# The clamp and the shift-and-mask of the float64 weights' conversion: once over 1024 columns or twice over 512

## The chip, the cores and the metric

The kernel runs on one core of one Trainium2 chip. The metric is the device time of one execution in microseconds (us). A core has TensorE (PE: matrix products; PEld: its weight loads), VectorE (DVE), ScalarE (ACT), GpSimd (POOL), and SyncE (SP), whose queue starts most of the transfers.

## The reference

Three layers follow each other: a cross read between tokens and state rows, a gated linear unit, and a soft mixture of experts. The expert weights and the attention are left out here but for their shapes; what the change touches are `w_gate`, `w_val` and `w_out`, which come as float64, since a float32 draw is multiplied by a float64 scalar.

```python
def _attn_ref(x, state):                  # x (8, 8, 512, 64), state (8, 8, 32, 64)
    a = softmax(scale * x @ state.T); xread = a @ state
    a2 = softmax(scale * state @ x.T); sread = a2 @ x
    return concatenate([xread, sread], axis=2)
def _moe_ref(x, w_gate, w_val, w_out, rms_g):   # x (4608, 512) -> 4352 rows here, d_ff 1536
    rms = np.sqrt(np.mean(x * x, axis=-1, keepdims=True) + 1e-06)
    xn = x / rms * rms_g
    g = xn @ w_gate
    silu = g * (1.0 / (1.0 + np.exp(-g)))
    val = xn @ w_val
    return (silu * val @ w_out).astype(np.float32)
def _moe2_ref(x, phi, w1, w2):            # 8 experts of 4 slots
    logits = x @ phi
    d = softmax over tokens; slot_input = d.T @ x
    slot_out[e] = np.maximum(slot_input[e] @ w1[e], 0.0) @ w2[e]
    c = softmax over slots; return c @ slot_out
```

## The kernel before, in words

The tokens are worked through in eight groups of 512 (one for each batch) and one of 256 (the sread rows). A group's attention is kept as the pair "weights A, state rows", so that the gate and value products of a group are A times (state rows times weight chunk): `sw` (L430 and on) multiplies the state rows by a chunk of 512 weight columns and splits the product into two parts (ScalarE L442, VectorE L443), `main_mm` multiplies A by them, L471 and L479 make silu times value, `h_T` (L490) turns it and `lg_mm` multiplies it by w_out @ phi, which `wphi_part` builds from converted rows of w_out (L632, L635, L639). The weights' chunk that `sw` reads is `W[gv, c]`, a tile of 128 x 4 x 512.

The weights arrive as the two 32-bit words of each float64 (`wload`, tile `raw`, 2 x 128 rows of 512 weights a load), and are rounded to float32 on the chip. There are 24 such half-chunks: 12 for the gate and value weights (out tile `w`), 6 of w_out's transpose and 6 of w_out (out tile `wo`); the last six are written to a tensor in the chip's memory for the tail. A conversion has two steps. `wconv_begin` is two ScalarE instructions over 1024 columns: the high word's magnitude (L184) and the scaled low word (L187). `wconv` is the rest: a clamp (VectorE, L200), a shift with a mask (VectorE, L204), a merge with the high word's upper bits (VectorE, L208), and an add of the rounded low word (GpSimd, L212). All four run on 512 columns at a time, first the one half, then the other.

What sets the order: the start-up, from the first load to the first group's norm, lies in a block whose order on each engine is that of the program text. It holds four conversions, each between pieces of the first group's attention, and on VectorE in this order: conversion, row maxima of the scores (L251) and of their transposes (L272, L273), conversion, sums and products of the softmax (L298 to L308), the split of the first product (L443), conversion, the two differences of A (L380), conversion, the split of the second product (L443), the norm's Newton steps (L409 to L422). GpSimd has the adds between the state's scaling (L227) and the state's mask product (L357, L365, L366). After the start-up a table (`at(unit, slot, function)`) sets the program text's order of conversions and all other pieces beside the main products; from it a scheduler makes each engine's order at compile time, by priority and readiness, so that neighbouring pieces interleave. In the steady stages one conversion belongs to a stage of 12 units.

Of the kernel before, what the change touches and what calls it, by code (L numbers as in the profile page):

```python
# [13 lines left out]
ALU = mybir.AluOpType  # L14
# [6 lines left out]
def kernel(  # L21
# [16 lines left out]
    nc = tc.nc  # L38
# [3 lines left out]
    DM = H * D  # L42
# [10 lines left out]
    big = ctx.enter_context(tc.tile_pool(name="big", bufs=1))  # L53
# [32 lines left out]

# [1 line left out]
    ident = small("ident", [P, P])  # L88
# [9 lines left out]

    # Bits of float64's high word, read as float32: the least and greatest that float32 holds.
    EXP_LO, EXP_HI = 2.0 ** -15, 122879.984375  # L100

    def keep_warm(n):
        """Products that nobody reads, so that a short wait doesn't slow the array's clock."""
        ps = mmps()
        for _ in range(n):
            tc.keep_in_program_order(nc.tensor.matmul(out=ps[:, :P], lhsT=ident, rhs=ident, start=True, stop=True))
# [3 lines left out]

# [1 line left out]
    XN, T = {}, {}  # L112
# [19 lines left out]

# [1 line left out]
    dram = ctx.enter_context(tc.tile_pool(name="dram", bufs=1, space=bass.MemoryType.DRAM))  # L134
# [57 lines left out]
    def wconv(n):  # L192
        for _ in range(n):
            if not begun:
                wconv_begin()
            gv, c, j, d2, dst, hi, rnd = begun.pop(0)
            a = dst.bitcast(I32)
            hs = [slice(0, 512), slice(512, 1024)]
            for h in hs:
                nc.vector.tensor_scalar(  # L200
                    out=dst[:, h], in0=dst[:, h], scalar1=EXP_LO, scalar2=EXP_HI,
                    op0=ALU.max, op1=ALU.min,
                )
                nc.vector.tensor_scalar(  # L204
                    out=a[:, h], in0=a[:, h], scalar1=3, scalar2=0x3FFFFFF8,
                    op0=ALU.logical_shift_left, op1=ALU.bitwise_and,
                )
                nc.vector.scalar_tensor_tensor(  # L208
                    out=a[:, h], in0=hi[:, h], scalar=-0x40000000, in1=a[:, h],
                    op0=ALU.bitwise_and, op1=ALU.bitwise_or,  # L210
                )
                nc.gpsimd.tensor_tensor(  # L212
                    out=a[:, h], in0=a[:, h], in1=rnd[:, h], op=ALU.add
                )
            if gv == 2:
                WOT[c, j] = d2
            if gv == 3:
                r0 = c * 512 + 2 * j * P
                nc.sync.dma_start(
                    out=w_out32[r0 : r0 + 2 * P, :].rearrange("(k p) d -> p k d", p=P), in_=d2  # L220
                )


# [1 line left out]
    def att_g(b):  # L225
# [177 lines left out]
    def rinv_from(g, ss, n):  # L403
        """(ss / DM + 1e-6) ** -0.5, by Newton's steps from the halved exponent."""
        y = small("rinv", [P, NT], bufs=3)[:, :n]
        v = small("rv", [P, NT])[:, :n]
        a = small("ra", [P, NT])[:, :n]
# [18 lines left out]

# [1 line left out]
    WP = {}  # L428
# [18 lines left out]

# [1 line left out]
    HH, HT, LGP = {}, {}, {}  # L449
# [60 lines left out]

# [1 line left out]
    sacc = small("sacc", [P, 1])  # L512
# [107 lines left out]

# [1 line left out]
    wphi_done, WPP = set(), {}  # L622

    def wphi_part(c, j):
        """phi' @ w_out' for half of the d_model rows of a 512-wide chunk; j = 1 ends the chunk."""
        wt = WOT.pop((c, j))
# [16 lines left out]

# [1 line left out]
    def sread_prep():  # L645
# [27 lines left out]
    def w_split(gv, c):  # L673
        """The weights' chunk in two float32r parts."""
        w = W.pop((gv, c))
        h, l = k8("wh", F32R), k8("wl", F32R)
# [6 lines left out]

# [1 line left out]
    EW = {}  # L685
# [14 lines left out]
    def prefetch(n, home=None):  # L700
        """Start the next n loads, in slots of `big` (home None) or of the experts' pool."""
        for _ in range(n):
# [23 lines left out]

# [1 line left out]
    def conv1(n=1):  # L728
# [43 lines left out]
    pinned.append(1)  # L772
# [1 line left out]
    def rinv(b):  # L774
# [24 lines left out]
    for s, units in enumerate(stages):  # L799
# [66 lines left out]
        else:  # L866
            g = s
            o = 4 if s == 1 else 0  # the first unit's place in the usual twelve
            if s == 1:
# [125 lines left out]

# [1 line left out]
    h_T(*pend[0])  # L997
# [59 lines left out]
    for k in range(4):  # L1057
        mm(ps[:, 32 * k : 32 * k + 32], sip[:, k * P : (k + 1) * P], r32)
    # each expert's inputs of its own slots, zero in the others'
    for e in range(NE):  # L1060
# [20 lines left out]
    def expert_in(p):  # L1081
        """The first products of two experts: slots of one have zeros in the other."""
        for j in range(2):
# [39 lines left out]
    def out_prep():  # L1123
        """Group 0's weights of the slots, in two parts, each four times."""
        ch = k8("ch", F32R)[:, 0, :P].rearrange("p (t s) -> p t s", s=32)
# [87 lines left out]

    # so_ps still has the four parts of each slot's sum; group 0 takes it as it is
    s4 = k8("s4", F32R)
# [88 lines left out]
```

## Time and profile before

| | us |
|---|---|
| runs, median (lowest to highest of 3) | 690.29 (690.04 to 691.79) |
| profiled execution, span | 691.4 |
| TensorE busy in it | 640.3 (93%) |
| VectorE, ScalarE, GpSimd busy | 407.7, 388.9, 129.1 |

A line of the timeline gives start, length, engine, line, operation, tile written and read, shapes, how many were merged into the line, and in brackets how long the engine stood idle before it and who released it. Instructions on one engine can overlap a little at their ends, so the length of two merged ones is less than twice one. PEclk is the clock that was granted to TensorE: 1.00 is 2.4 GHz, 0.50 is 1.2 GHz.

### The profile page before, as it was taken

Reading aid. Unit: us, or ns where it says so; the run is one execution under the profiler, and the core shown is the slowest. Engines: PE = TensorE matmul, PEld = TensorE weight load, DVE = VectorE, ACT = ScalarE, POOL = GpSimd, SP = SyncE. Lnnn points to the kernel's source line nnn. Section 1 sums busy time; section 2 is a strip of 40 time slices with the busy share of each in tenths; the row PEclk is TensorE's granted clock in tenths of the full one; section 3 lists DMA queues with packets and bytes.
Section 4 is the critical chain, followed back from the end, with each engine's and each line's share of the span. In section 5 each row is a group of like instructions: output and inputs, shape, how many; then the busy total and the mean of one; then the engine's idle time right before and its main releaser. Section 6 shows DMA issues by size and latency. Waiting matters only on the chain.

```text
span 691.4 us, 11529 instructions
## 1 busy us (share of the span) xinstructions
PE 640.3 (93%) x4560; PEld 410.6 (59%) x4560; DVE 407.7 (59%) x852; ACT 388.9 (56%) x632; POOL 129.1 (19%) x158
## 2 busy tenths in 40 slices
PE   6789988999989999999999999999999999999980
PEld 4346646456555766566676658665666676753350
DVE  6979996762687457554835673575455355342160
ACT  5477943754776459546764765496446366311170
POOL 2634554230032101110201021011000000002430
PEclk9799998999999999999999999999999999999995
DMA  9940246031042011203110320020081307999957
GB/s 349 404 193 2 101 152 236 1 129 63 1 156 96 5 47 77 96 5 122 45 53 1 122 92 1 19 105 31 1 309 58 122 1 257 326 334 382 344 186 331
DMA packets 33581, 92.55 MB, mean 134 GB/s; under 512 B 1912, under 2 KB 4088, under 8 KB 30712
## 3 DMA queue, kind: packets, MB, share of 16 engines
q1 hardware_dynamic: 33240, 91.76, 36.3%
q8 instruction: 36, 0.59, 0.4%
q14 instruction: 17, 0.14, 0.1%
q10 hardware_dynamic: 288, 0.07, 0.0%
HBM read 79.76 MB, written 12.06 MB: 133 GB/s over the span
## 4 chain that ended last, share of the span: by engine, by line
PE 75%; DVE 7%; ACT 5%; issue 1%; POOL 0%; DVEq 0%; ACTq 0%
PE mm L85 42%; PE misc L85 17%; PE misc L109 10%; PE lg L85 3%; PE so L85 2%; DVE wp L443 1%; DVE h L479 1%; ACT wp L442 1%; ACT L471 1%; DVE wo L200 1%; ACT sg L471 1%; DVE wo L208 1%; DVE rm L272 1%; ACT sT L285 0%; DVE wo L204 0%
## 5 line engine op out<-in xcount | busy, mean ns | idle before, releaser
L85 PE MATMUL mm<-wp,A 128*128 128x512 f32 x1152 | 304.9, 405 | 0.4 <-DVE h L479 0.4
L85 PEld LDWEIGHTS mm<-wp,A 128*128 128x128 f32 x1152 | 207.3, 189 | 64.1 <-issue 24.5
L479 DVE SCALAR_TENSOR_TENSOR h<-mm,rinv,sg 128x512 f32<-128x512 f32 x102 | 76.1, 747 | 131.1 <-PE mm L85 93.6
L471 ACT ACTIVATE sg<-mm,rinv 128x512 f32<-128x512 f32 x102 | 70.2, 690 | 81.0 <-PE mm L85 78.0
L85 PE MATMUL misc<-w,stTg 64*32 64x512 f32 x768 | 81.7, 618 | 17.6 <-DVE wp L443 7.5
L442 ACT CAST wp<-misc 128x512 fp32r<-128x512 f32 x96 | 51.7, 591 | 65.2 <-PE misc L85 63.1
L443 DVE TENSOR_TENSOR wp<-misc,wp 128x512 fp32r<-128x512 f32 x96 | 61.8, 682 | 26.6 <-ACT wp L442 26.1
L109 PE MATMUL misc<-ident,h 128*128 128x128 f32 x408 | 61.3, 277 | 1.9 <-DVE h L479 0.7
L490 ACT COPY hT<-misc 128x512 f32<-128x512 f32 x86 | 49.2, 580 | 24.6 <-PE misc L109 20.5
L109 PEld LDWEIGHTS misc<-ident,h 128*128 128x128 f32 x408 | 50.1, 142 | 18.2 <-DVE wp L443 3.3
L85 PEld LDWEIGHTS misc<-w,stTg 64*32 64x32 f32 x768 | 15.5, 106 | 67.7 <-issue 22.1
L308 POOL TENSOR_TENSOR a<-a,asum 128x1024 f32<-128x1024 f32 x7 | 13.4, 1917 | 132.4 <-issue 84.8
L471 ACT ACT_TABLE_LOAD x28 | 35.9, 1283 | 3.7 <-PE mm L85 3.2
L416 POOL TENSOR_TENSOR rinv<-ri,rs_magic 128x4 int32<-128x4 int32 (+1 forms) x9 | 1.8, 198 | 173.2 <-DVE ri L412 173.2
L397 ACT ACTIVATE misc<-misc 128x512 f32<-128x512 f32 x32 | 18.7, 585 | 26.9 <-PE misc L85 18.8
L212 POOL TENSOR_TENSOR w<-w,raw 128x512 int32<-128x512 int32 x20 | 28.1, 1418 | 27.6 <-ACT wp L442 7.2
L85 PE MATMUL mm<-wh,xsg 128*128 128x512 f32 x96 | 31.7, 399 | 0.0
L85 PE MATMUL misc<-bd,A 128*128 128x256 f32 x192 | 29.6, 292 | 1.5 <-DVE A L380 1.5
L212 POOL TENSOR_TENSOR wo<-wo,raw 128x512 int32<-128x512 int32 x18 | 24.8, 1387 | 32.7 <-DVE wo L208 23.3
L85 PE MATMUL lg<-hT,wphi 128*32 128x512 f32 (+1 forms) x216 | 27.4, 577 | 1.5 <-ACT hT L490 1.5
L85 PEld LDWEIGHTS misc<-bd,A 128*128 128x128 f32 x192 | 25.5, 191 | 5.1 <-DVE A L380 2.2
L85 PE MATMUL misc<-h,ET 128*32 128x512 f32 x204 | 26.4, 596 | 0.0
(196 smaller groups left out, 831.8 us busy)
## 6 DMA issues: line engine op xcount, KB each, us to landing
ew<-in_w_dram SPq DMA_DIRECT2D x27, 1024.0 KB, 8.1
xT<-in_x_t_dram SPq DMA_DIRECT2D x8, 1024.0 KB, 5.5
xn<-in_x_n_dram SPq DMA_DIRECT2D x8, 1024.0 KB, 7.7
raw<-in_w_val_dram SPq DMA_DIRECT2D x6, 1024.0 KB, 16.6
raw<-in_w_out_dram SPq DMA_DIRECT2D x6, 1024.0 KB, 5.0
out_dram<-ob SPq DMA_DIRECT2D x6, 1024.0 KB, 12.1
ew_w<-in_w_dram SPq DMA_DIRECT2D x5, 1024.0 KB, 10.4
raw<-in_w_gate_dram SPq DMA_DIRECT2D x4, 1024.0 KB, 14.2
```

Of the source, the lines that this page charges most:

```text
L85: nc.tensor.matmul(out=o, lhsT=lhsT, rhs=rhs, start=start, stop=stop)
L109: nc.tensor.transpose(o, i, ident)
L200: nc.vector.tensor_scalar(out=dst[:, h], in0=dst[:, h], scalar1=EXP_LO, scalar2=EXP_HI, op0=ALU.max, op1=ALU.min,)
L208: nc.vector.scalar_tensor_tensor(out=a[:, h], in0=hi[:, h], scalar=-0x40000000, in1=a[:, h], op0=ALU.bitwise_and, op1=ALU.bitwise_or,)
L212: nc.gpsimd.tensor_tensor(out=a[:, h], in0=a[:, h], in1=rnd[:, h], op=ALU.add)
L308: (eng or nc.gpsimd).tensor_tensor(out=a3, in0=a3, in1=asum.unsqueeze(2).to_broadcast([P, 32, 32]), op=ALU.mult)
L397: nc.scalar.activation(out=ps, in_=ps, func=AF.Square, accum_out=T[b, "ss"][:, t : t + 1])
L442: nc.scalar.copy(t[:, r, 0, :], ps)
L443: nc.vector.tensor_tensor(out=t[:, r, 1, :], in0=ps, in1=t[:, r, 0, :].bitcast(F32), op=ALU.subtract)
L471: nc.scalar.activation(out=sg, in_=ps, func=AF.Silu, scale=RINV[g][:, t : t + 1])
L479: nc.vector.scalar_tensor_tensor(out=HH[g, c][:, t, :], in0=ps, scalar=RINV[g][:, t : t + 1], in1=sg, op0=ALU.mult, op1=ALU.mult,)
L490: (nc.vector.tensor_copy if on_dve else nc.scalar.copy)(HT[g, c][:, :, t * P : (t + 1) * P], ps.rearrange("p (q n) -> p q n", q=4))
```

## The change

The clamp and the shift-and-mask are taken out of the loop over the two halves and run once over all 1024 columns, before it. The merge and the add stay in the loop. Each conversion has thus two VectorE instructions fewer (six become four), and both halves' clamp and shift come ahead of the first merge in the program text. The diff also drops comments and docstrings, which are not shown.

```diff
             a = dst.bitcast(I32)
             hs = [slice(0, 512), slice(512, 1024)]
+            nc.vector.tensor_scalar(
+                out=dst, in0=dst, scalar1=EXP_LO, scalar2=EXP_HI,
+                op0=ALU.max, op1=ALU.min,
+            )
+            nc.vector.tensor_scalar(
+                out=a, in0=a, scalar1=3, scalar2=0x3FFFFFF8,
+                op0=ALU.logical_shift_left, op1=ALU.bitwise_and,
+            )
             for h in hs:
-                nc.vector.tensor_scalar(
-                    out=dst[:, h], in0=dst[:, h], scalar1=EXP_LO, scalar2=EXP_HI,
-                    op0=ALU.max, op1=ALU.min,
-                )
-                nc.vector.tensor_scalar(
-                    out=a[:, h], in0=a[:, h], scalar1=3, scalar2=0x3FFFFFF8,
-                    op0=ALU.logical_shift_left, op1=ALU.bitwise_and,
-                )
                 nc.vector.scalar_tensor_tensor(
                     out=a[:, h], in0=hi[:, h], scalar=-0x40000000, in1=a[:, h],
                     op0=ALU.bitwise_and, op1=ALU.bitwise_or,
```

## Rows read from the trace of the kernel before

**Rows 1.** The page: busy us (share) xinstructions of each engine; TensorE's busy tenths

```profile
PE 640.3 (93%) x4560; PEld 410.6 (59%) x4560; DVE 407.7 (59%) x852; ACT 388.9 (56%) x632; POOL 129.1 (19%) x158
...
PE   6789988999989999999999999999999999999980
```

**Rows 2.** Stretches: length, then busy us of PE, PEld, DVE, ACT, POOL; PEclk; DMA

```profile
80.00:90.00 10.00, 10.00 (x60) 7.48 (x59) 10.00 (x15) 7.89 (x11) 6.20 (x5) 1.00 0.84 315
110.00:120.00 10.00, 8.27 (x103) 5.71 (x109) 6.55 (x11) 1.91 (x3) 5.96 (x4) 0.83 0.41 142
329.00:393.00 64.00, 62.46 (x478) 41.84 (x477) 37.44 (x80) 40.62 (x67) 8.18 (x8) 1.00 0.17 60
```

**Rows 3.** The clamp's line for gate and value weights: ns shortest/median/longest

```profile
L200 DVE TENSOR_SCALAR w<-w x24: 366/420/2151, 7.1 to 89.1; 128x512 f32<-128x512 f32 x24
```

**Rows 4.** Timeline of the start-up's second conversion, VectorE and GpSimd

```profile
15.38 0.42 DVE L200 TENSOR_SCALAR w<-w 128x512 f32<-128x512 f32 x1
15.83 0.43 DVE L204 TENSOR_SCALAR w<-w 128x512 int32<-128x512 int32 x1
16.29 0.69 DVE L208 SCALAR_TENSOR_TENSOR w<-raw,w 128x512 int32<-128x512 int32 x1
...
17.12 1.35 POOL L212 TENSOR_TENSOR w<-w,raw 128x512 int32<-128x512 int32 x1 [4.32 <-DVE w L208]
17.36 1.40 DVE L204 TENSOR_SCALAR w<-w 128x512 int32<-128x512 int32 x1
...
19.40 0.16 DVE L298 TENSOR_SCALAR rs<-s 128x2 f32<-128x2 f32 x1
...
19.56 1.29 POOL L212 TENSOR_TENSOR w<-w,raw 128x512 int32<-128x512 int32 x1 [1.09 <-DVE rs L298]
```

**Rows 5.** Timeline of the start-up's first conversion: an add and the second merge

```profile
9.41 1.47 POOL L212 TENSOR_TENSOR w<-w,raw_t 128x512 int32<-128x512 int32 x1
9.77 1.66 DVE L208 SCALAR_TENSOR_TENSOR w<-raw_t,w 128x512 int32<-128x512 int32 x1
```

**Rows 6.** Timeline of the start-up's end: third and fourth conversion and who waits

```profile
24.72 0.41 DVE L200 TENSOR_SCALAR w<-w 128x512 f32<-128x512 f32 x1
...
28.73 1.28 DVE L380 TENSOR_TENSOR A<-misc,A 128x512 fp32r<-128x512 f32 x2
...
34.24 1.28 POOL L212 TENSOR_TENSOR w<-w,raw 128x512 int32<-128x512 int32 x1 [1.09 <-DVE w L208]
...
35.58 1.07 PE L85 MATMUL misc<-w,stTg 64*32 64x512 f32 x10 [0.91 <-POOL w L212]
...
37.27 1.29 DVE L443 TENSOR_TENSOR wp<-misc,wp 128x512 fp32r<-128x512 f32 x2 [3.11 <-ACT wp L442]
```

**Rows 7.** Timeline of two conversions in the scheduler's order

```profile
57.93 0.76 DVE L200 TENSOR_SCALAR w<-w 128x512 f32<-128x512 f32 x2
...
58.61 0.75 DVE L204 TENSOR_SCALAR w<-w 128x512 int32<-128x512 int32 x2
...
59.28 0.68 DVE L208 SCALAR_TENSOR_TENSOR w<-raw,w 128x512 int32<-128x512 int32 x1
...
87.63 1.53 DVE L200 TENSOR_SCALAR w<-w 128x512 f32<-128x512 f32 x1
```

**Rows 8.** TensorE's gaps with VectorE last, and its clock by stretches (busy, PEclk, DMA)

```profile
94.53 1.06 PE L85 MATMUL misc<-w,stTg 64*32 64x512 f32 x7 [3.11 <-DVE e2T L318]
...
116.02 1.39 PE L85 MATMUL misc<-r,wpp 64*128 64x32 f32 x8 [1.73 <-DVE wpp L635]
...
117.00:123.00 6.00, 6.00 (x31) 0.50 0.05 20
...
191.38 1.31 DVE L204 TENSOR_SCALAR wo<-wo 128x512 int32<-128x512 int32 x1
...
192.95 1.09 PE L109 MATMUL misc<-ident,sT 128*128 128x128 f32 x8 [0.78 <-DVE xsT L350]
...
192.00:194.00 2.00, 1.22 (x12) 1.00 0.00 0
```

## The prediction

> **What bounds the kernel now.** The page's busy line and its forty slices come first [rows 1]: TensorE is busy for 93% of the span, and the slices (17.3 us each) in which it is below nine tenths are the first three, the sixth and seventh (86 to 121 us), the twelfth (190 to 207) and the last two. An edit on VectorE and GpSimd can only count where TensorE has a gap. The table by stretches [rows 2] says where VectorE could be the reason: from 80 to 90 us it is busy all the time beside a full TensorE; from 110 to 120 TensorE loses 1.7 of 10 us; in a middle stage (329 to 393) TensorE has 62.46 of 64 us and VectorE 37.44, with much room. The 24 conversions lie so: four in the start-up, whose order is written by hand, fourteen from 49 to 138 us, one at 188 us, five in the later stages, one to a stage.
>
> Next, the clamp's line, one instruction at a time [rows 3]: the median is 0.42 us for 512 columns, the longest 2.15. What makes an instruction long is seen in the start-up's second conversion [rows 4]. The first half's GpSimd add runs from 17.12 to 18.47 us; the second half's shift starts at 17.36 and lasts 1.40 us, to 18.76, which is the add's end and 0.29 us. VectorE's shift stands still while GpSimd's add runs. So does a merge that starts behind an add: at 9.77 us and 1.66 long, past an add that ends at 10.88 [rows 5].
>
> **The change, part by part.** Each conversion loses two VectorE instructions, and its first GpSimd add comes behind the whole clamp and shift. No wait on a DMA, no transfer and no instruction of ScalarE or TensorE is touched; the queue that is passed is GpSimd's, whose first add starts later.
>
> *Price of a wide instruction.* It is not in the trace. A clamp of 512 columns takes 0.42 us, a tensor_scalar of 2 columns 0.16 us [rows 4]: 0.51 ns a column, so 0.42 + 0.26 = 0.68 us for 1024. Bounds: 0.60 us (all but the columns overlaps the neighbour) and 0.84 us (two of 0.42).
>
> *Start-up conversions.* Here each instruction of a half needs the one before: starts 0.45 and 0.46 us apart [rows 4], 0.04 us beyond the duration. Before, counted from the clamp at 15.38: first merge at +0.91, first add's end +3.09, second add's end (20.85) +5.47, VectorE free at 19.40, +4.02. After: clamp and shift 0.72 us each, merges at +1.44 and +2.05, VectorE free at +2.66; the first add waits for the second merge and ends near +3.84, the second near +5.14. A conversion's own end gains only 0.33 us, its first half comes 0.75 us later, and VectorE is free 1.36 us sooner. The last is what counts, since VectorE's other work stands behind it:
> - First: its second merge no longer waits for the add, so the row maxima behind it could start 1.4 us sooner, until they wait for TensorE's scores; the second conversion starts near 14.4 instead of 15.38.
> - Third: between lie a small tensor_scalar and GpSimd's mask product, which now meet adds in another place; I keep a gain of 1.0 (24.72 to 23.7 [rows 6]).
> - Behind the third, the two differences of A run at 26.4 instead of 28.73 [rows 6]. The fourth could start at 27.6, but the third's second add runs to about 28.85 and holds the clamp or the shift: first merge near 30.1, last add's end near 33.85 instead of 35.52.
>
> TensorE's last products of the second weight chunk start at 35.58, at that add's end, after 0.91 us idle [rows 6]; all that follows hangs on them. Gain 1.7 us; bounds 0.9 (the collisions cost what the third and fourth gain) and 2.4 (none happens).
>
> *Conversions under the scheduler's order.* Here the halves are already interleaved: two clamps in 0.75 us, two shifts in 0.75, the first merge 1.35 us behind the first clamp [rows 7]. Independent neighbours start 0.33 us apart, so most of the fixed part is overlapped; a wide instruction on which the next depends has nothing to overlap with: 0.72 + 0.72 = 1.44 us against 1.35. That is 0.09 us worse. Where the adds of the conversion before still run (the clamp at 87.63 takes 1.53 us instead of 0.42 [rows 7]), the first half waits for one add and the second for the other; the wide clamp takes the first wait and the wide shift the second, again about +0.1. From 65 to 92 us six conversions lie on a busy VectorE, ahead of the stall of 3.11 us that ends at 94.53 with VectorE's copy e2T [rows 8]: 6 x 0.1 = +0.6 us on the path. Bounds: -0.8 (other ready work fills the gaps; four starts of 0.33 become two of 0.60, -0.13 each) and +1.5 (the wide price is 0.84). Two more lie ahead of the stall of 1.73 us that ends at 116.02 with VectorE's sum wpp: +0.2, bounds -0.3 and +0.5. The other four of 95 to 138 us and the two before 60 lie beside a TensorE with other work: nothing, and +0.1 each if that cover goes.
>
> Of the fixed part the Trainium skill has another rule (VectorE: DVE Perf Modes, "The DRAIN you can't avoid"): an operation starts only when the one before has left the pipeline, and the count of operations should be kept low. By it a conversion saves 2 x (0.84 - 0.68) = 0.32 us everywhere, and the six are worth -1.9 instead of +0.6. The interleaved halves, two in 0.75 us and not in 0.84, speak against it.
>
> A rule that speaks against the change is the Trainium skill's on the port pair (SBUF — State Buffer, "Who interferes with whom"): VectorE and GpSimd take it for a whole instruction, and the later one is blocked. A clamp twice as wide then holds GpSimd up to 0.27 us longer; an add of 1.47 us behind a shift, against 1.29 elsewhere [rows 4, 5], agrees in kind. By it the start-up would gain 1.4 instead of 1.7, 688.9 in all.
>
> *The conversion at 188 us.* Its second shift stands 1.31 us at 191.38 beside its own first add; behind it on VectorE is the copy xsT, for which TensorE stands 0.78 us before 192.95 [rows 8]. The wide shift is done before any add: -0.8; bounds -0.8 and 0. The five later ones lie in stages where VectorE has 26 us to spare: 0, bounds -0.1 and +0.1 each.
>
> **Sum.** -1.7 + 0.6 + 0.2 - 0.8 = -1.7 us. The profiled execution's span is 691.4 us, 1.1 above the median of the three runs (690.29) and inside their spread; with -1.7 it is 689.7, and the median 688.6 us.
>
> **The rivals.**
> - *VectorE's busy stretch gets shorter, not longer.* The scheduler puts ready work, TensorE's evictions among it, into the new gaps between clamp and shift, or the fixed part is saved (two of 0.42 become one of 0.68). The six are then worth -0.8 to -1.9, the stalls before 94.53 and 116.02 shrink, and TensorE's clock may stay up behind one: from 117 to 123 us, behind the second, it was granted 0.50 of full speed, 1.2 GHz [rows 8], some 3 us lost. For: VectorE is the last to arrive at both stalls. Against: both evictions stand behind waits on adds that remain. 690.3 - 1.7 - 0.8 - (0.8 to 1.9) - (0 to 3): 683 to 687, about 685.3. That the fixed part is saved is what the Trainium skill's section on the DRAIN would have.
> - *Slower: a new TensorE gap between 95 and 140 us.* With fewer and longer instructions the scheduler's order moves, and an eviction that TensorE needs falls behind a wide clamp or shift that waits for two adds, some 2.6 us. Price: a gap like the one before 116.02, 1.73 us, and the low clock behind it, 3 us: 4.7 less the 1.7 gained, 693.3. It decides where such an eviction is the last that TensorE waits for and the clock falls behind it; the gap of 0.78 us before 192.95 was followed by full speed [rows 8]. For: two such places exist already. Against: most of this stretch has TensorE fully busy, with a backlog that covers a late eviction.
> - *The start-up gain is swallowed.* The collisions cost all of it, or the last products wait for ScalarE's squares or TensorE's own queue. For: a conversion's own end gains only 0.33 us. Against: VectorE is idle for 3.11 us before its next work at 37.27 [rows 6], waiting for those products through ScalarE. About 690.3.
> - *The edit doesn't do what it says*: a wide instruction at one column a cycle, near 1.2 us. Nothing speaks for it, since the layout is as contiguous; 2 in 100, counted with the slower case.
>
> **How the numbers follow.** Forecast case, own range 687.3 to 689.9: 0.45. Shorter stretch, about 685.3: 0.25. Slower, about 693.3: 0.17. Swallowed, about 690.3: 0.13. 0.3% is 2.1 us, about what a measurement of this kernel can tell from no change, so faster means below 688.2; of the forecast case 0.18 lies there and 0.27 within. Faster 0.18 + 0.25 = 0.43; same 0.27 + 0.13 = 0.40; slower 0.17. From the middle of the shorter case to the lower half of the slower one, with about 0.2 left out: 685.2 to 692.5.
>
> **What would show it.** In the start-up: no shift of 1.4 us, the last products of the second chunk near 33.9 instead of 35.58, wide instructions near 0.68 us. From 65 to 92: the first merge 1.44 us behind an unblocked clamp, or other work between (the first rival). No shift beside its own add near 190. A TensorE gap of over 1.5 us where none is now, one of the two gone, or those last products still at 35 would make the prediction wrong.

## The result, and the profile after

The changed kernel is slower: median 694.29 us (690.38 to 695.55, 13 runs) against 690.23 us (689.25 to 693.20, 13 runs), ratio 1.0060, interval 1.0046 to 1.0073. That is 4.1 us more where 1.7 less were forecast, and outside the range. One of the changed kernel's 13 executions took 690.38, the other twelve 694.12 to 695.55; it was not traced, and why it was spared is open.

One number has to be set right before traces are compared. A run's time is its span and 1.7 to 2.0 us (694.39 for the span of 692.4 of the profile after). The profile of before has a span of 691.4, so that execution took about 693.3 us, at the upper end of its kernel's runs and 3 us above their median. The kernel before was therefore profiled once more (e8_before_again: span 688.5, time 690.39), and that trace is the one that "before" means from here on. Where a lead is given, the n-th main product of A is taken in both traces, and its start after is subtracted from its start before; a negative lead is a loss. The expectations below call this the shift of a trace; elsewhere "shift" is the shift-and-mask instruction. Leads are given at the time in the later kernel.

> The kernel before once more, for a second profile: whether the low clock from 117 to 123 us in its first profile (span 691.4 us, at the upper end of its runs) is in each execution. If it is, the span is near 691; if it isn't, near 688.5, and the changed kernel is to be compared with that.

The page's busy line of the changed kernel [rows 1]: VectorE is busy for 404.9 us, against 407.7 in the first profile of before and 405.6 in the second, in 48 instructions fewer. TensorE is busy for longer than in either (641.9 us; 640.3 and 638.1).

```profile
PE 641.9 (93%) x4560; PEld 410.3 (59%) x4560; DVE 404.9 (58%) x804; ACT 388.5 (56%) x632; POOL 132.0 (19%) x158
```

The changed kernel's timeline in the start-up [rows 4, 6] (start, length, engine, line, operation; the clamp is L199 here, the shift L203, the merge L208, the add L212):

```profile
15.13 0.68 DVE L199 TENSOR_SCALAR w<-w 128x1024 f32<-128x1024 f32 x1
15.85 0.69 DVE L203 TENSOR_SCALAR w<-w 128x1024 int32<-128x1024 int32 x1
16.57 1.29 DVE L208 SCALAR_TENSOR_TENSOR w<-raw,w 128x512 int32<-128x512 int32 x2
...
28.71 1.68 DVE L203 TENSOR_SCALAR w<-w 128x1024 int32<-128x1024 int32 x1
...
34.15 1.07 PE L85 MATMUL misc<-w,stTg 64*32 64x512 f32 x10 [0.20 <-POOL w L212]
```

The wide instruction costs what was forecast (0.68 and 0.69 us, starts 0.72 apart, first merge at +1.44), no shift stands beside its own add, and the last products of the second chunk start at 34.15 instead of 35.58. Up to 64 us the changed kernel is 1.3 to 1.4 us ahead. Then it falls behind. The stretches of the changed kernel (columns as in [rows 2]):

```profile
64.00:72.00 8.00, 6.53 (x40) 4.16 (x39) 7.07 (x15) 2.45 (x3) 2.86 (x2) 1.00 0.18 39
72.00:80.00 8.00, 5.63 (x23) 1.66 (x22) 7.92 (x12) 6.92 (x10) 3.33 (x3) 0.77 0.22 92
90.00:100.00 10.00, 9.03 (x58) 4.39 (x56) 10.00 (x14) 7.66 (x10) 6.25 (x4) 1.00 0.31 107
110.00:120.00 10.00, 8.32 (x99) 5.89 (x97) 8.74 (x11) 4.12 (x4) 5.03 (x4) 1.00 0.64 239
120.00:126.00 6.00, 5.58 (x38) 2.63 (x37) 1.77 (x5) 2.83 (x5) 1.08 (x1) 0.72 0.17 71
```

The same stretches of the kernel before, second profile:

```profile
64.00:72.00 8.00, 8.00 (x48) 5.73 (x47) 7.30 (x24) 6.11 (x9) 3.10 (x3) 1.00 0.01 2
72.00:80.00 8.00, 7.34 (x35) 3.65 (x35) 8.00 (x15) 7.44 (x10) 5.24 (x4) 1.00 0.00 0
90.00:100.00 10.00, 6.86 (x28) 3.25 (x28) 10.00 (x20) 4.86 (x7) 4.84 (x4) 0.78 0.31 107
110.00:120.00 10.00, 9.61 (x120) 5.79 (x119) 6.55 (x15) 3.65 (x6) 7.78 (x4) 1.00 0.34 115
120.00:126.00 6.00, 5.86 (x45) 2.70 (x44) 4.65 (x10) 5.45 (x9) 0.02 (x1) 1.00 0.11 46
```

TensorE loses from 64 to 80 us (12.16 us busy instead of 15.34, at a clock of 0.77 in the second half), wins back from 90 to 100 (9.03 instead of 6.86, full clock instead of 0.78), and loses again from 110 to 126. The leads say the same: +1.3 at 63 us, -4.3 at 82, -2.2 at 109, -4.9 at 131, -5.4 at 151, and -3.6 at 227, since 1.9 us come back at the conversion at 188 us. Behind that nothing changes any more.

*From 64 to 78 us.* VectorE, GpSimd and TensorE of the changed kernel. L418, L419 and L422 are the Newton steps of the group's norm on 4 columns; L471 and L479 make silu times value from their result:

```profile
64.21 0.69 DVE L199 TENSOR_SCALAR w<-w 128x1024 f32<-128x1024 f32 x1
...
66.34 0.68 DVE L208 SCALAR_TENSOR_TENSOR w<-raw,w 128x512 int32<-128x512 int32 x1
66.57 2.86 POOL L212 TENSOR_TENSOR w<-w,raw 128x512 int32<-128x512 int32 x2 [3.14 <-PE misc L109]
...
66.94 1.26 DVE L419 SCALAR_TENSOR_TENSOR ra<-ra,rv 128x4 f32<-128x4 f32 x1
68.24 1.22 DVE L422 SCALAR_TENSOR_TENSOR rinv<-ra,rinv 128x4 f32<-128x4 f32 x1
...
70.29 3.03 PE L85 MATMUL mm<-wp,A 128*128 128x512 f32 x12 [1.47 <-ACT sg L471]
...
74.02 1.28 DVE L443 TENSOR_TENSOR wp<-misc,wp 128x512 fp32r<-128x512 f32 x2
75.22 0.68 DVE L208 SCALAR_TENSOR_TENSOR w<-raw,w 128x512 int32<-128x512 int32 x1
...
77.71 2.04 PE L85 MATMUL misc<-w,stTg 64*32 64x512 f32 x10 [1.74 <-POOL w L212]
...
93.34 2.22 PE L85 MATMUL misc<-w,stTg 64*32 64x512 f32 x16
```

The kernel before, second profile, same place:

```profile
67.41 0.15 DVE L422 SCALAR_TENSOR_TENSOR rinv<-ra,rinv 128x4 f32<-128x4 f32 x1
67.48 0.69 DVE L208 SCALAR_TENSOR_TENSOR w<-raw,w 128x512 int32<-128x512 int32 x1
...
68.51 4.38 PE L85 MATMUL mm<-wp,A 128*128 128x512 f32 x18
...
75.57 1.07 PE L85 MATMUL misc<-w,stTg 64*32 64x512 f32 x10 [0.21 <-POOL w L212]
...
94.57 2.24 PE L85 MATMUL misc<-w,stTg 64*32 64x512 f32 x12 [3.14 <-DVE e2T L318]
```

Here the scheduler lays the Newton steps and a conversion's instructions into each other, one by one. Before, six VectorE instructions of the conversion cover six steps, and the last step stands ahead of the last merge. After, only four instructions are left to alternate with, the last two steps come behind both merges, and so beside the adds that the merges released: 1.26 and 1.22 us in place of 0.15. The silu waits for them, TensorE waits for the silu (1.47 us). In the next conversion the second merge (75.22) comes behind three other instructions (one L479 and the two L443 at 74.02), its add ends late, and TensorE waits 1.74 us for it. The wait for VectorE's copy e2T, 3.14 us before 94.57, is not there after the change: TensorE comes to that place 4.7 us later and finds the copy ready. That wait and the half clock behind it are what is won back from 90 to 100 us.

*From 111 to 119 us.* The two neighbouring conversions ahead of the sum wpp (L635), after the change:

```profile
113.39 3.35 POOL L212 TENSOR_TENSOR wo<-wo,raw_t 128x512 int32<-128x512 int32 x2 [3.49 <-DVE wo L208]
...
113.77 1.80 DVE L199 TENSOR_SCALAR wo<-wo 128x1024 f32<-128x1024 f32 x1
115.61 1.68 DVE L203 TENSOR_SCALAR wo<-wo 128x1024 int32<-128x1024 int32 x1
...
119.34 1.07 PE L85 MATMUL misc<-r,wpp 64*128 64x32 f32 x8 [1.68 <-DVE wpp L635]
```

And before, second profile:

```profile
111.10 5.27 POOL L212 TENSOR_TENSOR wo<-wo,raw_t 128x512 int32<-128x512 int32 x2 [4.03 <-DVE wo L208]
...
111.49 0.76 DVE L200 TENSOR_SCALAR wo<-wo 128x512 f32<-128x512 f32 x2
...
115.88 1.07 PE L85 MATMUL misc<-r,wpp 64*128 64x32 f32 x8 [0.39 <-DVE wpp L635]
```

In both an add of the first conversion is ready 0.4 us before the second one's clamp. Before, VectorE runs its four halves in 0.42 us each, behind a merge that ends at 111.56, and the add waits (two adds take 5.27 us); the sum wpp comes almost in time (0.39 us). After, the adds run first, clamp and shift stand still for one each (1.80 and 1.68 instead of 0.69), and TensorE waits 1.68 us and then drops to half clock (PEclk 0.50 from 121 to 124 us). The profile of [rows 8], with its gap of 1.73 us and 0.50 from 117 to 123 us, was an execution of the kernel before in which the adds had also got in first.

### The profile page after: what moved, and what is told of

It is laid out like the page before. It is cut to its first block, busy times and chain, and to the rows that moved or that the text cites. A ratio compares the mean times of both kernels' runs of the same rounds, so it can differ in the third digit from the quotient of the medians.

```text
span 692.4 us, 11484 instructions
## 1 busy us (share of the span) xinstructions
PE 641.9 (93%) x4560; PEld 410.3 (59%) x4560; DVE 404.9 (58%) x804; ACT 388.5 (56%) x632; POOL 132.0 (19%) x158
## 4 chain that ended last, share of the span: by engine, by line
PE 75%; DVE 7%; ACT 4%; issue 2%; POOL 0%; DVEq 0%; ACTq 0%; POOLq 0%
PE mm L85 42%; PE misc L85 17%; PE misc L109 10%; PE lg L85 3%; PE so L85 2%; DVE wp L443 2%; DVE h L479 1%; ACT wp L442 1%; DVE w L208 1%; ACT L471 1%; ACT sg L471 1%; DVE wo L199 1%; DVE rm L272 1%; ACT sT L285 0%; DVE wo L208 0%
## 5 line engine op out<-in xcount | busy, mean ns | idle before, releaser
L85 PE MATMUL mm<-wp,A 128*128 128x512 f32 x1152 | 308.5, 408 | 1.8 <-ACT sg L471 1.5
L479 DVE SCALAR_TENSOR_TENSOR h<-mm,rinv,sg 128x512 f32<-128x512 f32 x102 | 76.1, 748 | 134.2 <-PE mm L85 95.1
L471 ACT ACTIVATE sg<-mm,rinv 128x512 f32<-128x512 f32 x102 | 70.2, 689 | 86.9 <-PE mm L85 80.6
L443 DVE TENSOR_TENSOR wp<-misc,wp 128x512 fp32r<-128x512 f32 x96 | 61.8, 683 | 27.1 <-ACT wp L442 26.6
L212 POOL TENSOR_TENSOR w<-w,raw 128x512 int32<-128x512 int32 x20 | 30.4, 1538 | 29.3 <-ACT misc L397 6.3
L212 POOL TENSOR_TENSOR wo<-wo,raw 128x512 int32<-128x512 int32 x18 | 25.2, 1417 | 34.4 <-DVE wo L208 19.3
```

Source lines behind the costliest of these rows:

```text
L85: nc.tensor.matmul(out=o, lhsT=lhsT, rhs=rhs, start=start, stop=stop)
L212: nc.gpsimd.tensor_tensor(out=a[:, h], in0=a[:, h], in1=rnd[:, h], op=ALU.add)
L443: nc.vector.tensor_tensor(out=t[:, r, 1, :], in0=ps, in1=t[:, r, 0, :].bitcast(F32), op=ALU.subtract)
L471: nc.scalar.activation(out=sg, in_=ps, func=AF.Silu, scale=RINV[g][:, t : t + 1])
L479: nc.vector.scalar_tensor_tensor(out=HH[g, c][:, t, :], in0=ps, scalar=RINV[g][:, t : t + 1], in1=sg, op0=ALU.mult, op1=ALU.mult,)
```

## The experiments

All kernels below but three (e4, e16 and e8, the kernel before itself) are one text: a list says which of the 24 conversions use the wide clamp and shift, the others go by halves as before. Counted from 0 they lie so: 0 to 3 in the start-up, 4 at 49 us, 5 at 57, 6 at 64, 7 at 69, 8 to 11 from 74 to 92, 12 and 13 from 95 to 102, 14 and 15 from 109 to 115, 16 and 17 from 124 to 136, 18 at 188, 19 to 23 later; the times move by some us from kernel to kernel. In these kernels' traces the clamp stands at L204, the shift at L207, the merge at L217, the add at L221, and lines behind them are 9 higher. The comments in the diffs are added here.

```diff
+            wide = cnt["conv"] in WIDE
+            cnt["conv"] += 1
+            if wide:
+                prep(dst, a)              # clamp, shift over 1024
             for h in hs:
+                if not wide:
+                    prep(dst[:, h], a[:, h])
```

| kernel | WIDE | median us | ratio to before (interval) |
|---|---|---|---|
| e1_startup | 0-3 | 690.08 | 0.9999 (0.9989 to 1.0009) |
| e2_stage0 | 4-17 | 698.64 | 1.0134 (1.0111 to 1.0157) |
| e3_late | 18-23 | 688.13 | 0.9973 (0.9961 to 0.9984) |
| e4_newton | all, see below | 695.25 | 1.0069 (1.0055 to 1.0083) |
| e5_all_but_two | all but 6, 7 | 692.88 | 1.0032 (1.0020 to 1.0044) |
| e6_first_of_two | 6 | 694.37 | 1.0056 (1.0038 to 1.0074) |
| e7_second_of_two | 7 | 690.41 | 0.9999 (0.9987 to 1.0011) |
| e9_c_and_d | 14, 15 | 692.67 | 1.0035 (1.0021 to 1.0048) |
| e10_all_but_four | all but 6, 7, 14, 15 | 690.04 | 0.9992 (0.9981 to 1.0003) |
| e11_one_wide | 15 | 692.04 (one run) | |
| e12_both_ends | 0-3, 18-23 | 687.17 | 0.9959 (0.9944 to 0.9973) |
| e13_ends_and_w | the same and 4, 5, 8-11 | 690.26 | 0.9998 (0.9988 to 1.0007) |
| e14_ends_and_a_b | both ends and 12, 13 | 688.03 | 0.9972 (0.9959 to 0.9986) |
| e15_ends_and_e_f | both ends and 16, 17 | 687.86 | 0.9971 (0.9961 to 0.9982) |
| e16_abreast | 14, 15, see below | 689.75 | 0.9995 (0.9984 to 1.0007) |
| e17_ends_and_57 | both ends and 4, 5 | 688.83 | 0.9979 (0.9967 to 0.9992) |
| e18_ends_and_74_92 | both ends and 8-11 | 688.93 | 0.9985 (0.9975 to 0.9995) |

**By places.** The first three runs divide the kernel into start-up, the middle (49 to 138 us) and the rest.

> The wide clamp and shift in the four start-up conversions alone; the other twenty run by halves as before. The order behind the start-up is that of the kernel before. Theory A (the start-up gains what it gained in the changed kernel, where the last products of the second chunk start at 34.15 instead of 35.58 us, and the loss arises later): 1.4 us less than before, 688.8, with the shift kept to the end. Rival B (the gain is spent by TensorE's clock or by a later wait whatever the later conversions do): within 0.5 us of before, 690.

> The wide clamp and shift in the fourteen conversions from 49 to 138 us alone. Theory A (the whole loss arises in this stretch, most of it at 64 to 78 us, where two Newton steps of the group's norm land behind both merges and beside the adds): the changed kernel's +4.0 and the 1.4 that the start-up gives, so 5.4 us more than before, 695.6, and in the timeline near 66 to 70 us two small steps of about 1.2 us each. Rival B (the loss comes from each wide instruction's exposed end, some 0.1 us a conversion): at most 1.5 us more, 691.7. Rival C (the loss lies in the later stages): no change.

> The wide clamp and shift in the conversion at 188 us and the five later ones alone. Theory A: no loss here; the traces of before and after show main products from 170 to 226 us moving from +2.7 to +0.8 us, so a gain of 0.8 (the shift beside its own add is gone) to 1.9: 688.3 to 689.4. Rival C (the later stages' new order costs): more than 690.7.

The loss is in the middle alone, 1.3%, more than in the whole change; the late conversions gain 0.27%. The middle's time is 3 us above what theory A gave. In its trace 1.9 us are gone at 50 us, ahead of the first wide conversion (51.4), and 1.5 are still gone at 57: TensorE's clock was at 0.50 from 35 to 45 us, and at 1.00 there in the trace of before. Whether the other four executions had this isn't known. The start-up by itself shows nothing in the time, as rival B said, although its trace has the shorter order. In that trace the main products are still 1.1 us ahead at 560 us; the lead is lost at 654.68 us, where TensorE stands 1.30 us until expert weights have arrived (`ew`, by DMA). The traces of before and of e12 below don't have this wait, so it may be that execution's chance. The late gain, of the size that theory A gave, lies at one place, the conversion at 188 us: in the changed kernel both of its instructions are done before any add [rows 8].

```profile
190.59 0.69 DVE L199 TENSOR_SCALAR wo<-wo 128x1024 f32<-128x1024 f32 x1
...
191.87 0.68 DVE L203 TENSOR_SCALAR wo<-wo 128x1024 int32<-128x1024 int32 x1
...
193.66 1.28 DVE L208 SCALAR_TENSOR_TENSOR wo<-raw,wo 128x512 int32<-128x512 int32 x2
```

**The Newton steps.** e4 has everything wide, but conversion 6 is queued on VectorE behind the last Newton step, so that no step can meet its adds. In this kernel the step is L436 and the add L225.

```diff
+            hold = ExitStack()
+            if cnt["conv"] - 1 == 6:
+                hold.enter_context(tc.issue_after(NEWT[1].ins))   # last Newton step of the group
             if wide:
                 prep(dst, a)
```

> The changed kernel, but the VectorE instructions of the one conversion that is interleaved with the second group's norm (64 us) are queued behind the norm's last Newton step, so that none of these steps can stand beside the adds. Theory A: the group's factors are ready near 65.5 instead of 69.5 us, TensorE's gaps of 1.47 and 1.74 us before 70.3 and 77.7 and the low clock behind them go, and the time falls by 4 to 6 us to 688 to 690. Rival B (exposed ends of the wide instructions everywhere): 693.5 to 694.5, as the changed kernel. Rival D (the conversion itself is then too late for the second chunk's product): the gap before 77.7 stays, 692 to 694.

```profile
66.27 0.16 DVE L436 SCALAR_TENSOR_TENSOR rinv<-ra,rinv 128x4 f32<-128x4 f32 x1
...
75.08 3.30 POOL L225 TENSOR_TENSOR w<-w,raw 128x512 int32<-128x512 int32 x2 [2.54 <-ACT w L186]
...
76.74 3.64 PE L86 MATMUL misc<-w,stTg 64*32 64x512 f32 x12 [3.08 <-POOL w L225]
```

The steps are cured (the last at 66.27, 0.16 us) and nothing is won: conversion 7's clamp and shift meet conversion 6's adds, the scheduler puts evictions between and behind them, its merges come at 74.28 instead of 71.82, and TensorE waits 3.08 us for its add. The time, 695.25, is above every expectation; rival D's account, the conversion too late, is the nearest. So the steps were one way into this loss, not the only one; common to both is that the add for which TensorE waits comes late, because merges wait behind other work.

> The changed kernel, but the two conversions at 64 to 76 us (the two row halves of one weight chunk) run their clamp and shift by halves as before; the other 22 are wide. Theory A2 (the loss is the scheduler's order in that one place: with fewer VectorE instructions of the conversion, two Newton steps fall behind both merges, and the second conversion's last merge falls behind three evictions, so that the add that TensorE waits for comes 2 us later, and the low clock follows): the order there is as before, TensorE's gap before 77.7 goes, and with the 2.0 us of the late conversions and up to 1 from the start-up the time is 687 to 688.5. Rival B (exposed ends of the wide instructions): 693.5 to 694.5 less a seventh, so over 693.

> Only the conversion that is interleaved with the second group's Newton steps (64 us) is wide; the other 23 run by halves. Theory A2: the order behind it moves as in the changed kernel (two Newton steps behind the merges; the next conversion's second merge behind three evictions although that conversion itself runs by halves), so 4 to 7 us more than before: 694 to 697. Rival B: 0.1 us, so 690.2.

> Only the next conversion (69 us), the one whose adds TensorE waits for at 75.5 us, is wide; the other 23 run by halves. VectorE's order is that of before, with two instructions for four. Theory A2: as before within 0.5 us, 690 to 690.7: a wide clamp and shift cost 0.1 us as such. Rival E (the wide clamp's and shift's waits for the adds of the conversion before make the awaited add late by themselves): more than 692.

With 6 and 7 by halves the lead at 78 us is -0.16, where the changed kernel comes to -4.3: this loss is gone, and half of the time's increase is still there (1.0032). Most of it arises at 111 to 126 us (1.4 us go between 82 and 100, of which 0.8 come back by 104). Neither expectation of e5's time was met (692.88). Conversion 6 alone makes the loss by itself (1.0056; its steps take 1.26 and 1.22 us, TensorE waits 1.08 us for the silu and 3.60 us for an add); 7 alone makes none in the time (its trace loses 1.6 us by 78 us, with a low clock from 75.8, and has them back by 97).

**Who gets the port.** The place before the sum wpp, alone, and its converse.

> Only the two neighbouring conversions ahead of the phi sum at 110 to 119 us (the fifteenth and the sixteenth, counted from the start) have the wide clamp and shift; all the others go by halves. The two VectorE stretches are the only order that differs from the kernel before. Theory F (at this place the form itself decides who gets the port that VectorE and GpSimd share: behind a wide pair the waiting GpSimd add gets in at the next conversion's clamp, behind four overlapping halves VectorE mostly keeps it until the merges): the second wide clamp takes about 1.80 us and the shift about 1.68, TensorE waits about 1.7 us ahead of the phi products and drops to half clock within 5 us of it, and the time is 2 to 3 us above a kernel with everything by halves: 692 to 693, ratio 1.002 to 1.004. Theory G (who gets in is chance that the form doesn't touch, since the add also got in between the halves in two of six traces): clamps in some executions 0.68, the time that of the kernel before within 0.2%, 689.5 to 691.5.

> All conversions wide but four, which go by halves: the two at 65 to 78 us and the two at 110 to 119 us. The converse of the run before. Theory F: the wait ahead of the phi products is about 0.4 us again and no low clock follows it, so it is 2 to 3 us less than with all but two wide (692.9): 689.8 to 690.9; with the later gain of 1.1 to 1.8 us whole and the start-up's 0 to 1.4, down to 688. Theory G: 692 to 693.5, as with all but two wide. A third, theory H (the loss comes with the two wide conversions at 95 to 110 us, which shift what follows): 692 to 693.5 as well, with the wait of 0.4 us and the loss earlier than 110 us.

> Only the second of the two neighbouring conversions ahead of the phi sum (the sixteenth) is wide. Up to its clamp the instructions are those of the kernel before. If the wide clamp itself loses the port (one form of theory F): clamp 1.80, shift 1.68, wait of TensorE ahead of the phi products about 1.7 us. If what decides is the stretch before it, the wide pair and merges of the fifteenth (the other form), or chance (G): clamp 0.68, shift 0.69, the add waits some 3 us, and TensorE's wait is about 0.4 us. A single trace can't tell the last two apart.

Time and trace are those of theory F. Two wide conversions there, in an order that is otherwise that of the kernel before, cost 0.35%; taken out of e5, they give 692.88 - 690.04 = 2.8 us back. Over all traces: with both wide (after, e2, e4, e5, e9) TensorE's wait is 1.67 or 1.68 us, five times in five, each time with a low clock behind it. With both by halves, in 13 traces, it is 0.38 to 0.75 us in ten, with no low clock, and 1.71 to 1.94 in three (the first profile of before, e6, e14), each with a low clock behind it. So by halves it is a chance, and wide it came in every trace. (The one execution of the changed kernel at 690.38 may have been without it.) e11, with 15 alone wide, met neither of its expectations; its VectorE and GpSimd show the moment:

```profile
110.49 3.94 POOL L221 TENSOR_TENSOR wo<-wo,raw_t 128x512 int32<-128x512 int32 x2 [3.92 <-DVE wo L217]
...
110.87 0.69 DVE L204 TENSOR_SCALAR wo<-wo 128x1024 f32<-128x1024 f32 x1
111.59 1.67 DVE L207 TENSOR_SCALAR wo<-wo 128x1024 int32<-128x1024 int32 x1
```

The add is ready at 110.49, the wide clamp starts behind it and runs unblocked, and the shift, which needs the clamp's result and can't overlap it, finds the port taken. With both wide the add already gets in at the clamp. e16 asks whether another order of the same wide instructions avoids it: clamp 14, clamp 15, shift 14, shift 15, then the merges.

```diff
+            if n_conv == 14:
+                clamp(dst)
+                last = clamp(dst2)                  # of conversion 15
+                with tc.issue_after(last.ins):
+                    s1 = shift(a)
+                with tc.issue_after(s1.ins):
+                    shift(a2)
+            elif n_conv == 15:
+                pass                            # done with 14
```

> As with only the two conversions ahead of the phi sum wide (692.67), but in the order clamp, clamp, shift, shift, so that no wide instruction follows the one that it waits for; the merges come behind the four. If the dependence lets the add in: the four run in 0.68 to 0.72 us each, no add comes between them, TensorE waits less than 0.8 us ahead of the phi products, no low clock follows within 5 us, and the time is that of the kernel before or a little less, 689.3 to 690.5. If the width as such lets it in: a clamp or shift of 1.6 to 1.8, and 692 to 693.

Its timeline (the clamp is L205, the shift L210, the merge L236, the sum L663):

```profile
110.04 0.69 DVE L205 TENSOR_SCALAR wo<-wo 128x1024 f32<-128x1024 f32 x1 [1.06 <-ACT wo L185]
110.65 1.29 DVE L210 TENSOR_SCALAR wo<-wo 128x1024 int32<-128x1024 int32 x2
...
113.26 0.68 DVE L663 TENSOR_TENSOR wpp<-misc,wpp 64x512 f32<-64x512 f32 x1
...
114.54 1.07 PE L86 MATMUL misc<-r,wpp 64*128 64x32 f32 x8
```

TensorE doesn't wait at all, and the loss is gone (0.9995). The order is a cure; that the dependence is the cause isn't shown by it, since the merges come later here and no add was ready while the four ran.

**The rest of the middle.** Both ends wide and the middle by halves is faster than both kernels, by 0.41% against before (five executions, 686.82 to 688.66).

> Wide at both ends (the four conversions of start-up and the last six, 186 us and later), by halves in between (45 to 140 us), where the order is that of the kernel before. If the losses are those of 64 to 78 and 110 to 126 us alone and the late gain is its own: 687.3 to 688.6, ratio 0.996 to 0.998, faster than both kernels. If the late gain of the kernel with only the last six wide was its run's chance, 689.5 to 690.5.

From there to e10 are ten more conversions and 2.9 us, to which the prediction had given a few tenths. Three runs divide them.

> Both ends wide, and in the middle the six conversions of the gate and value weights at 48 to 64 us and at 78 to 92 us; the two at 65 to 78 us and the six of w_out by halves. If the open 2.9 us lie in these six (by the prediction's own step they cost 0.2 us each, 0.6 in all with the two left out here; the shift of the trace with all but four wide went from 1.4 to 1.05 us at 78 us and to 0.16 at 100 us, 1.3 us of loss): 688.4 to 690. If not: 686.8 to 687.6.

> Both ends wide, and in the middle only the first two conversions of w_out at 98 to 102 us. The trace with all but four wide won 0.7 us back between 100 and 106 us, so nothing is lost here by it: 686.8 to 687.6. If the open 2.9 us lie here: 689 to 690.

> Both ends wide, and in the middle only the last two conversions of w_out at 128 to 136 us, after the phi sum's first chunk. The trace with all but four wide lost 0.5 us from 125 to 145 us: 687.4 to 688.2. If the open 2.9 us lie here: 689 to 690; if nothing does: 686.8 to 687.4.

The six of the gate and value weights hold it (3.1 us); 12 and 13, or 16 and 17, cost 0.7 to 0.9 us each by the medians, which the intervals don't tell from nothing.

> Both ends wide, and in the middle only the conversions at 49 and at 57 us. If the loss comes from the one at 57 us (VectorE's two products of the weight by the gate fill the place between shift and merge, so both merges come behind them, the adds 1.4 us later for the first half, and the first small step of the token norm at 62.5 us runs beside an add: 1.04 us in place of 0.17; the last small step, the silu and the conversion at 69 us follow 0.5 us later; TensorE waits 0.86 us at 74 us in place of 0.45): the first small step again takes about 1.04, TensorE's wait at 74 us is 0.8 to 0.9 us, in some executions a low clock follows at 75 us, and the time is 689.3 to 690.4. If it comes from the four at 74 to 92 us: 686.8 to 687.8.

> Both ends wide, and in the middle only the four conversions at 74 to 92 us. If the loss comes from the one at 57 us: the small steps and TensorE's wait at 74 us as in the kernel with both ends wide (0.45), and 686.8 to 688. If it comes from these four: 689.3 to 690.4.

Neither expectation was met as it stood: by the medians both parts cost, 1.7 and 1.8 us. The interval of e18 just clears that of e12, that of e17 overlaps it a little. For the conversion at 57 us, e17 has the mechanism that was expected: both splits of the product (L452) stand ahead of both merges, where by halves one merge comes first; the adds come later, and the first small step of the norm runs beside one.

```profile
63.03 1.04 DVE L418 TENSOR_SCALAR rv<-ss 128x4 f32<-128x4 f32 x1 [0.77 <-ACT misc L406]
...
74.48 1.04 PE L86 MATMUL misc<-w,stTg 64*32 64x512 f32 x2 [0.86 <-POOL w L221]
```

The same two lines of e12, where the conversion goes by halves:

```profile
62.85 0.17 DVE L418 TENSOR_SCALAR rv<-ss 128x4 f32<-128x4 f32 x1 [1.09 <-ACT misc L406]
...
73.43 1.04 PE L86 MATMUL misc<-w,stTg 64*32 64x512 f32 x2 [0.45 <-POOL w L221]
```

That is 0.4 us of wait; e13's trace has a low clock from 75.7 us on besides (PEclk 0.79 in 72 to 80 us), e10's, with the same wait, has none. The executions of e13 lie in clusters (688.4 and 688.6; 689.8 to 690.3; 691.3 and 691.4), which would fit with low clocks in some, but of each kernel only one execution was traced. For the four from 74 to 92 us, e18 shows VectorE taking two conversions abreast, with four merges in a row, and the copy e2T behind them:

```profile
86.24 4.67 DVE L217 SCALAR_TENSOR_TENSOR w<-raw,w 128x512 int32<-128x512 int32 x4
...
92.88 1.93 PE L86 MATMUL misc<-w,stTg 64*32 64x512 f32 x8 [4.83 <-DVE e2T L327]
```

TensorE waits 4.83 us there, 2.94 in e12, and its clock is 0.50 from 90 to 100 us (0.66 in e12). The lead over e12 goes from +0.7 to -1.7 over this stretch.

**The account.** Taken as a chain, each kernel with more of the wide form than the last, the medians go: before 690.2; both ends wide -3.0 (687.17); ten of the middle +2.9 (690.04); the two ahead of wpp +2.8 (692.88); 6 and 7 +1.4 (694.29). They add up because each is a difference to the one before, and the order of the steps matters: 6 alone costs 3.9 us, and as the last step of the chain 6 and 7 cost 1.4, since a TensorE that came late from 78 us finds less to wait for at 90 to 100 us. e2, all of the middle and no end, is 4.4 us above after, though the ends are worth 3.0; the 1.4 us between may be the low clock in the start-up, and stay open.

## Why the prediction was wrong, point by point

The sum's two terms at the ends, -2.5 us, came out as -3.0 (e12); its terms in the middle, +0.8, came out as +7.1.

- *The price of a wide instruction.* Right: 0.68 and 0.69 us, starts 0.72 apart, first merge at +1.44.
- *Start-up, -1.7.* Right in kind: 1.43 us at the last products (34.15; 33.9 was forecast), still 1.3 at 64 us. Its pieces were smaller than said: the second conversion starts at 15.13 (14.4 was forecast), the third at 24.14 (23.7), and the small step L298 takes 1.26 us beside the first add, which the sum left out, so that VectorE is some 0.5 us sooner behind the second conversion and not 1.36. The fourth conversion's shift was held by the add as described (1.68 us at 28.71). In the time, the four alone are not to be seen (0.9999); with the late ones they may be (687.17 against 688.13, intervals that overlap).
- *The conversion at 188 us, -0.8.* Right sign, too small: in e3's trace the lead rises by 1.1 us at 193 and by 1.8 up to 223, and its ratio gives 1.9. The bound 0.8 took the wait before the copy xsT alone; in the second profile of before TensorE also stands 0.54 us at 188.80, and neither wait is there after.
- *The six conversions from 65 to 92 us, +0.6; the two before 60, nothing.* This step failed. It priced each conversion as if its instructions kept their places and only grew by 0.09 us, and put the whole cost on one path, the stall that ends at 94.53 with e2T. Their exposed ends are as small as that (e7: nothing in the time). But with two instructions fewer the scheduler's order changes, and what falls behind what costs 1.7 to 3.9 us (e17, e18, e6) instead of tenths: Newton steps behind merges and beside adds (6), a merge behind three other instructions (7, when 6 is wide), the merges behind both splits of the product (5), four merges ahead of e2T (10, 11). In the changed kernel TensorE waits for the silu and the adds up to 78 us (1.47 and 1.74 us), a place that the sum had no term for, and not for e2T at all. The bound of +1.5 was made from prices only, and by its own price is too small: two instructions of 0.84 put the first merge at 1.76 instead of 1.35 us, 0.41 a conversion, 2.5 for six. The remark that the halves "are already interleaved" held the warning: the halves were what the small steps were interleaved with.
- *The two ahead of 116 us, +0.2, bounds -0.3 and +0.5.* This step failed too: 2.8 us. The sum had the clamp and shift waiting for the adds in either form ("the first half waits for one add and the second for the other"). In ten of thirteen traces by halves they don't wait, the add does; both wide, they waited in five of five (1.80 and 1.68 us).
- *The base of the sum.* "1.1 above the median" set the span beside the runs' times; with the 1.9 us around it, the profiled execution was some 3.0 above the median, and what made it so was the gap and the low clock of [rows 8]. The stall that the text counts as part of the kernel is there in three of the thirteen traces by halves; the change made it the rule.
- *The rival "slower: a new TensorE gap between 95 and 140 us"* (0.17) was the nearest: 693.3 against 694.29, by order, with a wait for adds and a low clock. Its place was half right: the gap before wpp was named as existing, not as the one to come; and 64 to 78 us lies outside its stretch.
- *Rival one* (the fixed part is saved, 685.3). No run gave that gain. By the Trainium skill's rule (VectorE: DVE Perf Modes, "The DRAIN you can't avoid") the six would have won 1.9 us. The same section of the Trainium skill adds that an operation that isn't held starts earlier, and the halves agree (0.33 us apart, 0.42 long): there was little fixed part left to save. VectorE's busy time fell by 0.7 us against the second profile of before and by 2.8 against the first; none of it reached the end of the middle stages.
- *The port.* The Trainium skill (SBUF — State Buffer, "Who interferes with whom") says that VectorE and GpSimd take the shared pair for a whole instruction and that whichever issues first blocks the other. The long instructions above agree in their length (1.80 us is 0.69 and 1.1 beside an add that began 0.4 us earlier). Not so the order: before, the add is ready at 111.10, while a merge still runs, and four VectorE instructions that start at 111.49 and later go ahead of it. There the measurement decides.

## What to carry over

Fewer, longer instructions are not a local change where a scheduler fills gaps: before pricing them, look at what the short ones are interleaved with, and who waits for those neighbours. Ahead of the sum wpp, the waiting add got in at the wide clamp or at the shift that waits for it, in six traces of six; which of width and wait lets it in isn't shown. The add or small step that TensorE waits for should be kept off that place. Merge only where the order is fixed or the engine has slack: here the two ends gain 3.0 us (687.17) and the middle gives 7 back.

## What was not expected of the hardware

- A step on 128 x 4 values, 0.15 to 0.17 us alone, takes 1.02 to 1.26 us beside a GpSimd add (L409, L419 and L422 after), while evictions from TensorE's products keep their 0.68 to 0.75 us there (L443 and L479 at 73 to 74 us).
- Ahead of the sum wpp, with an add ready, four overlapping halves kept the port in ten of thirteen traces, and in the other three they lost it, though merge, add and clamp start at the same distances from each other to a few nanoseconds (add 0.38 to 0.39 us ahead of the clamp in all). What decides isn't known.
- A wait of TensorE of 1.36 to 1.94 us before the products of wpp was followed by half clock in all nine traces that have it, and one of 0.75 or less in none of eleven.
